# A fused attention and PReLU kernel: the order of the first loads, and which output tiles are computed in the first two stages

## The chip, the cores and the metric

The kernel runs on one core of a Trainium2 chip. The metric is the time of one execution on the device in microseconds (us), the median of several runs. TensorE is called PE, VectorE DVE, ScalarE ACT, GpSimd POOL, SyncE SP; PEld is the loading of weights into PE.

## The reference

Linear attention for 8 batches of 8 heads, 576 tokens and 64 columns a head, then a two-layer network with a learned leaky ReLU over all 4608 tokens:

```python
kv  = np.einsum('bhsd,bhse->bhde', k, v)
out = np.einsum('bhsd,bhde->bhse', q, kv)
rms = np.sqrt(np.mean(out * out, axis=-1, keepdims=True) + 1e-06)
attn = out / rms * g_norm                        # (8, 8, 576, 64)
x = attn.transpose(0, 2, 1, 3).reshape(4608, 512)
h = x @ w_in                                     # w_in (512, 2048)
g = np.maximum(h, 0.0) + alpha * np.minimum(h, 0.0)
y = g @ w_out                                    # w_out (2048, 512)
```

Everything comes and goes as float32; inside, the matmuls take 16-bit values.

## The kernel before

**Blocks and units.** The 4608 tokens are cut into nine blocks (w) of W = 512. For a block the hidden layer has NF = 16 units (g) of 128 hidden columns. A unit (`m1_group`) is four 128x512 matmuls into one PSUM bank (`m1_mm`, over the four 128-row pieces of x) and an evacuation (`m1_evac`): ACT writes relu(-h), DVE combines it with h into `gt`. The output of a block has four tiles (a) of 128 tokens; each is a chain of 16 matmuls, one for each g (`y_mm`), and `y_out` copies it out of PSUM and has SP issue two stores.

**Heads and batches.** A batch has 576 tokens, so blocks and batches don't line up: block 1 takes the last 64 tokens of batch 0 and 448 of batch 1, block 2 the last 128 of batch 1 (the "tail") and 384 of batch 2. q, k and v arrive by POOL's queue, each in two loads (`load`: the long one with five rows a partition, the short one with four), changed to 16 bits on the way. `regroup` puts heads side by side. `step_kv` makes kv for two or four pairs of heads: five matmuls of 128x128 for each pair.

**Two ways to make x.** Blocks 0 and 1 keep x with the columns on the partitions: `step_t` transposes q on PE, `step_ot` multiplies by kv, `ssq_mm` sums squares over a head by a matmul with a mask, ACT makes 1/rms by Ln and Exp, and `norm` multiplies on DVE. For batch 0, whose k, q and v come in halves of four heads, the second half goes in two column halves (`half_ot`, `half_ssq`). From block 2 on (NB_PE = 2) the tokens are on the partitions: `tile_a` multiplies, `tile_b` sums on DVE, `tile_c` has ACT and POOL make the factor `rg`, `tile_d` multiplies on DVE (`xrow`) and has SP transpose the result by DMA into `xm`. `phase_steps` hands these pieces out to the units of the block before, one tile a unit, with the lags between a, b and d in `lags`. The tail of batch 1 is made the first way (`step_tail_ot`, `step_tail_ssq`) and is written straight into `xm(2)`.

**The order.** Every engine's instructions run in the order in which the source issues them (`manual_schedule`); nothing is reordered. The start, block 0 and the second stage are written out by hand. `keep_warm(n)` issues n matmuls whose result nobody reads. `load_rest` issues the weights and batch 1. In the second stage, `ahead` multiplies block 0's output tiles `ys` while block 1's x is made: three tiles are done there, of the fourth only g 0 to 3 (`LATER = 4`); its other twelve matmuls follow in block 1's units. In the main loop a unit of block w carries four matmuls of block w-1's tiles.

**PSUM.** There are eight banks: h0, h1, h2, o0, o1, o2, s, y. A tile that takes a bank waits until the last reader of the tile before has ended.

**POOL and SP.** POOL issues all loads of q, k, v and weights in its own order, between its copies and the `rg` products; `gate` copies make it wait, at units 2 and 11 of block 1, for q's transpose and for xm(2). SP issues the stores and the transposes.

Of the kernel before, what the change touches and what calls it, by code (L numbers as in the profile page):

```python
# [9 lines left out]
FP32 = mybir.dt.float32  # L10
# [7 lines left out]
def kernel(  # L18
# [11 lines left out]
    nc = tc.nc  # L30

    B, H, S, D = q.shape
# [57 lines left out]
    def zero_rest(st):  # L90
        nc.vector.memset(st[REM:P, :, TPP, :], 0.0)
# [15 lines left out]
    def load(b, nm, h0=0, h1=H):  # L107
        load_part(b, nm, True, h0, h1)
        load_part(b, nm, False, h0, h1)

    def regroup(b, nm, h0=0, h1=H, eng=None):
        (eng or nc.vector).tensor_copy(  # L112
            out=bufs[b % NBUF][nm][:, :, h0:h1, :].rearrange("p t h d -> p h t d"),
            in_=stages[b % NBUF][nm][:, h0:h1],
        )
# [12 lines left out]
    ident = const_p.tile([P, P], FP32, name="ident")  # L128
    make_identity(nc, ident[:])
    HH = H // 2  # L130
    for h0 in (0, HH):
        for nm in "qkv":
            load(0, nm, h0, h0 + HH)

    mask32 = const_p.tile([P, P], FP32, name="mask32")
# [10 lines left out]
    nc.vector.memset(eps_t[:], 1e-6)  # L146
    ident16 = const_p.tile([P, P], FP16, name="ident16")
    nc.vector.tensor_copy(out=ident16[:], in_=ident[:])

    g2col = const_p.tile([P, 1], FP32, name="g2col")  # L150
    nc.sync.dma_start(out=g2col[0:64, :], in_=g_norm[:].unsqueeze(1))
# [35 lines left out]
    def load_rest():  # L187
        for i in range(WQ):
            load_w_in(i)
        for nm in "kvq":  # L190
            zero_rest(stages[1][nm])
        load(1, "k")
        load_w_out(0)
        load(1, "q")
        load(1, "v")
        for i in range(1, WQ):
            load_w_out(i)


# [158 lines left out]
    def step_tail_ssq(i, pool):  # L358
        ot_ps, sq = ots.pop(("tail", i))
        ssq_ps = pool[0].tile([P, JT, TAIL], FP32, name="ssq_ps", tag=pool[1])  # L360
        nc.tensor.matmul(out=ssq_ps[:], lhsT=mask16[:], rhs=sq[:], start=True, stop=True)
        rstd = attn_p.tile([P, JT, TAIL], FP32, name="rstd")
        nc.scalar.activation(
            out=rstd[:], in_=ssq_ps[:], func=AF.Ln, bias=eps_t[:], scale=inv_d,
        )
        nc.scalar.activation(out=rstd[:], in_=rstd[:], func=AF.Exp, bias=0.0, scale=-0.5)
        nc.vector.scalar_tensor_tensor(
            out=xm(NB_PE)[:, i * JT : (i + 1) * JT, 0:TAIL], in0=ot_ps[:], scalar=g2col[:],
            in1=rstd[:], op0=ALU.mult, op1=ALU.mult,
        )  # L370
# [13 lines left out]
            out=qtms[b][:], in_=bufs[b % NBUF]["q"][:].rearrange("p t h d -> p (t h d)"),  # L384
        )

    n_tile = [1]

    def next_o():
        n_tile[0] += 1  # L390
# [49 lines left out]
    def phase_steps(w):  # L440


        if w >= NW:
            return []
        todo = [(b, t) for b in range(NB_PE, min(B, w + 1)) for t in range(NT)
                if (b, t) not in done and b * S + t * P < (w + 1) * W]
        done.update(todo)
        steps = []

        kv_at = {NB_PE: 3, NB_PE + 1: 6, NB_PE + 2: 2}.get(w, 0)  # L450
        n = {NB_PE: 4, NB_PE + 1: 2}.get(w, 0)
        steps += [([], [], []) for i in range(n)]

        lags = (0, 1, 3) if w == NB_PE else (0, 1, 2)
        if w in (NB_PE + 1, NB_PE + 2):
            k = [b for b, t in todo].index(w)
            todo[k:k] = [None] * (3 if w == NB_PE + 1 else 1)
        for i in range(len(todo) + lags[2]):
            a, b, d = (
                [todo[i - k]] if 0 <= i - k < len(todo) and todo[i - k] else [] for k in lags  # L460
            )
            begin = [lambda x=x: tile_b(*x) for x in b] + [lambda x=x: tile_d(*x) for x in d]
            mid = [lambda x=x: tile_c(*x) for x in b]
# [66 lines left out]
    def spread_g():  # L530
# [7 lines left out]

    O2 = (ps_o, "o2")
    keep_warm(10)  # L540
    regroup(0, "q", 0, HH)
    nc.vector.tensor_scalar(
        out=diag[0:D], in0=ident[0:D, 0:D], scalar1=g2col[0:D], scalar2=None, op0=ALU.mult,
    )
    step_t(0, 0, H_POOL[0])
    step_t(0, 1, H_POOL[1], nc.scalar)
    regroup(0, "k", 0, HH)
    load_rest()
    keep_warm(8)
    step_kv(0, 0, 2)  # L550
    keep_warm(2)
    step_ot(0, 0)
    step_ot(0, 1)
    keep_warm(1)
    regroup(0, "q", HH, H)
    ssq_mm(0, 0)
    step_t(0, 2, H_POOL[2])
    step_t(0, 3, H_POOL[0])
    alpha_ps = ps_h.tile([P, NF], FP32, name="alpha_ps", tag="h1")
    nc.tensor.matmul(  # L560
        out=alpha_ps[:], lhsT=alpha_row[:], rhs=ident[0:NF, 0:NF], is_transpose=True,
# [4 lines left out]
    nc.vector.tensor_scalar(  # L566
        out=beta_sb[:], in0=alpha_ps[:], scalar1=-1.0, scalar2=1.0, op0=ALU.mult, op1=ALU.add,
    )
    ssq_mm(0, 1)
    regroup(0, "k", HH, H)  # L570
    spread_g()
    norm(0, 0)
    keep_warm(2)
    step_kv(0, 2, 4)
    keep_warm(2)
    load_batch(2)
    half_ot(0, (ps_s, "s"))
    norm(0, 1)
    half_ot(1, (ps_y, "y"), nc.vector)
    first = [ps_h.tile([P, W], FP32, name="h_ps", tag=f"h{g}") for g in range(3)]  # L580
    first += [ps_o.tile([P, W], FP32, name="h_ps", tag=f"o{g}") for g in range(2)]
    half_ssq(0, O2)
    for g in range(4):
        m1_mm(first[g], 0, g, (0,))
    for g in range(4):
        if g == 2:
            half_ssq(1, O2)
        m1_mm(first[g], 0, g, (1,))
    for i in range(2):
        for c in (2, 3):  # L590
            for g in range(4):
                m1_mm(first[g], 0, g, (c,), slice(i * HW, (i + 1) * HW))
                if (i, c) == (1, 3):
                    m1_evac(first[g], 0, g)
        if i == 0:
            m1_mm(first[4], 0, 4, (0, 1))
    m1_mm(first[4], 0, 4, (2, 3))
    m1_evac(first[4], 0, 4)
    others = {5: (ps_s, "s"), 6: (ps_y, "y"), 7: O2, 11: (ps_o, "o0"), 12: (ps_o, "o1"),
              13: (ps_s, "s")}  # L600
    for g in range(5, NF):
        m1_group(0, g, others.get(g))

    LATER = 4
    ys = [
        ps_h.tile([P, W], FP32, name="ya", tag="h2"),
        ps_o.tile([P, W], FP32, name="yb", tag="o0"),
# [4 lines left out]
    def ahead(g0, g1, tiles=range(TPW)):  # L614
        for g in range(g0, g1):
            for a in tiles:
                if a < TPW - 1 or g < LATER:
                    y_mm(ys[a], 0, a, g)

    S_POOL = (ps_s, "s")  # L620
    O1 = (ps_o, "o1")
    regroup(1, "k")
    ahead(0, 3)
    regroup(1, "q")
    step_t(1, 0, S_POOL)
    step_t(1, 1, O1, nc.scalar)
    step_t(1, 2, H_POOL[0])
    step_t(1, 3, H_POOL[1], nc.scalar)
    ahead(3, 4, range(2))
    step_kv(1, pool=S_POOL)  # L630
    ahead(3, 4, range(2, TPW))
    step_ot(1, 0, O1)
    step_ot(1, 1, H_POOL[0])
    step_ot(1, 2, H_POOL[1], nc.vector)
    ahead(4, 5)
    ssq_mm(1, 0, S_POOL)
    ahead(5, 7)
    ssq_mm(1, 1, S_POOL)
    norm(1, 0)
    ahead(7, 9)  # L640
    step_ot(1, 3, O1, nc.vector)
    norm(1, 1)
    ssq_mm(1, 2, S_POOL)
    ahead(9, 12)
    ssq_mm(1, 3, S_POOL)
    norm(1, 2)
    regroup(2, "q")
    transpose_q(2)
    ahead(12, 13)
    step_tail_ot(0, H_POOL[1])  # L650
    ahead(13, 15)
    norm(1, 3)
    step_tail_ssq(0, S_POOL)
    ahead(15, NF)
    for a in range(TPW - 1):
        y_out(ys[a], 0, a, nc.vector if a == 1 else None)

    LOAD_G = 6
    n_group[0] = 0
    for w in range(1, NW):
        steps = phase_steps(w + 1)
        for g in range(NF):
            if g == LOAD_G and 4 < w + 2 < B:
                load_batch(w + 2)
            a, part = divmod(g, TPW)
            parts = range(part * TPW, (part + 1) * TPW)
            if w == 1:  # L670
                a, y = TPW - 1, ys[TPW - 1]
                parts = [LATER + g] if LATER + g < NF else []
            begin, mid, end = steps.pop(0) if steps else ([], [], [])
            for f in begin:
                f()
            m1_group(w, g, [H_POOL[0], S_POOL, H_POOL[2], H_POOL[1]][g % 4] if w == 1 else None)
            for f in mid:
                f()
            if 0 in parts:
                pool, tag = ((ps_y, "y"), (ps_s, "s"))[a % 2]  # L680
                y = pool.tile([P, W], FP32, name="y_ps", tag=tag)
            for gg in parts:
                y_mm(y, w - 1, a, gg)
            if NF - 1 in parts:
                y_out(y, w - 1, a)
            for f in end:
                f()
            if (w, g) == (1, 0):
                regroup(2, "k", eng=nc.gpsimd)
            if (w, g) == (1, 2):  # L690
# [63 lines left out]
```

## Time and profile before

| | |
|---|---|
| median of 7 runs | 294.23 us (293.4 to 294.68) |
| the profiled execution | 294.13 us, its span 292.0 us |
| mean granted PE clock | 0.997 |
| busy: PE, PEld, DVE, ACT, POOL | 96%, 47%, 58%, 52%, 34% |
| w_in's first quarter issued, landed | 9.30, 16.9 us |
| first h of block 0 | 17.21 us |
| first y matmul (second stage) | 31.64 us |
| first h of block 1 | 49.10 us |
| first h of block 2 | 68.86 us |
| last of batch 2's loads landed | 53.6 us |

The span is the time from the first to the last instruction; 2.1 us lie around it. The profile gives the start of each PE instruction well, but its end is modelled and overlaps the next one; distances are best taken from start to start. A line of the timeline gives start, duration, engine, line of the source, operation, output and inputs, shape, count, and in brackets the idle time ahead of it with what ended it. The chain of waits follows the last instruction back to what released it at each step.

### The profile page before, as it was taken

What the parts mean: (1) busy time and instruction counts of PE and PEld (TensorE: products, weight loads), DVE (VectorE), ACT (ScalarE), POOL (GpSimd) and SP (SyncE); (2) the same over time, 40 slices, a digit from 0 to 9 for tenths busy, and PEclk for the clock granted to TensorE, in tenths of its full rate; (3) what the DMA queues carried; (4) which work ended last, traced back from release to release, by engine and by line L of the source; (5) the groups of instructions that cost most, each with busy time, mean ns of one, the idle gap of its engine ahead of it and who ended that gap; (6) DMA issues with size and microseconds to landing.
All of it is one profiled execution on the core that took longest, in us unless ns stands there. A gap on an engine that the chain in (4) does not pass through costs nothing.

```text
span 292.0 us, 4287 instructions
## 1 busy us (share of the span) xinstructions
PE 281.0 (96%) x1551; PEld 137.7 (47%) x1551; DVE 169.3 (58%) x261; ACT 152.8 (52%) x297; POOL 99.8 (34%) x111
## 2 busy tenths in 40 slices
PE   5999989998999999999999999999999999999994
PEld 2454444543454454455445544554445444444443
DVE  4669837787667576447744864488448644444300
ACT  1558457584656565448644754466448544444210
POOL 8923410684448128324743373324003200000000
PEclk9999999999999999999999999999999999999998
DMA  7999999999899826991699179944212311212133
GB/s 89 183 208 202 199 206 198 189 197 181 127 150 183 180 29 96 204 209 25 107 206 206 41 116 173 199 56 86 50 36 56 81 36 38 48 46 48 40 72 72
DMA packets 66228, 35.54 MB, mean 122 GB/s; under 512 B 32784, under 2 KB 61728, under 8 KB 66208
## 3 DMA queue, kind: packets, MB, share of 16 engines
q0 software_dynamic: 29664, 18.35, 45.3%
q1 hardware_dynamic: 36384, 16.80, 29.0%
q8 instruction: 12, 0.20, 0.3%
q10 hardware_dynamic: 160, 0.13, 0.2%
q14 instruction: 8, 0.07, 0.1%
HBM read 36.71 MB, written 9.44 MB: 158 GB/s over the span
## 4 chain that ended last, share of the span: by engine, by line
PE 76%; DMA 15%; POOL 4%; DVE 2%; issue 1%; ACT 1%; POOLq 0%; DVEq 0%
PE y_ps L505 38%; PE h_ps L478 33%; DMA w_in_sb<-in_moe_w_in_dram 5%; DMA vst<-in_v_dram 5%; DMA w_out_sb<-in_moe_w_out_dram 4%; PE kv_ps L245 2%; PE otm_ps L397 2%; DMA xm<-xrow 1%; DVE gt L487 1%; POOL w_in_sb L165 1%; DVE xrow L430 1%; POOL qst L97 0%; DVE ss L409 0%; POOL vst L102 0%; POOL vst L97 0%
## 5 line engine op out<-in xcount | busy, mean ns | idle before, releaser
L487 DVE SCALAR_TENSOR_TENSOR gt<-m_sb,beta_sb,h_ps 128x512 f16<-128x512 f32 x144 | 105.6, 744 | 75.1 <-ACT m_sb L485 74.5
L485 ACT ACTIVATE m_sb<-h_ps 128x512 f32<-128x512 f32 x144 | 85.4, 597 | 87.6 <-PE h_ps L478 86.4
L505 PE MATMUL y_ps<-w_out_sb,gt 128*128 128x512 f16 (+1 forms) x528 | 128.8, 373 | 0.0
L478 PE MATMUL h_ps<-xm,w_in_sb 128*128 128x512 f16 x448 | 115.0, 379 | 0.8 <-DMA xm<-xrow 0.8
L505 PEld LDWEIGHTS <-gt 128*128 128x128 f16 x592 | 57.6, 98 | 64.6 <-DMA w_out_sb<-in_moe_w_out_dram 0.2
L478 PEld LDWEIGHTS <-w_in_sb 128*128 128x128 f16 x584 | 55.8, 98 | 62.1 <-issue 2.3
L421 POOL TENSOR_TENSOR rg<-ss,g_all 128x512 f32<-128x512 f32 (+1 forms) x30 | 31.3, 1042 | 78.5 <-ACT ss L419 70.5
L478 PE MATMUL h_ps<-xt,w_in_sb 128*128 128x512 f16 (+1 forms) x136 | 30.6, 366 | 0.1
L515 ACT COPY y_sb<-y_ps 128x512 f32<-128x512 f32 (+1 forms) x32 | 18.4, 576 | 15.9 <-PE y_ps L505 15.9
L409 DVE TENSOR_REDUCE ss<-sqm_sb 128x8 f32<-128x512 f32 (+1 forms) x30 | 20.5, 683 | 10.5 <-ACT sqm_sb L403 10.5
L430 DVE TENSOR_TENSOR xrow<-otm_ps,rg 128x512 f16<-128x512 f32 (+1 forms) x30 | 20.5, 682 | 3.7 <-POOL rg L421 3.7
L403 ACT ACTIVATE sqm_sb<-otm_ps 128x512 f32<-128x512 f32 (+1 forms) x30 | 17.7, 591 | 6.3 <-PE otm_ps L397 6.3
L112 POOL COPY ksb<-kst 128x2560 f16<-128x2560 f16 x6 | 13.9, 2324 | 15.7 <-DMA kst<-in_k_dram 15.7
L112 POOL COPY qsb<-qst 128x2560 f16<-128x2560 f16 x5 | 11.6, 2316 | 10.4 <-issue 10.1
L397 PEld LDWEIGHTS <-qtm 128*128 128x128 f16 x120 | 9.1, 98 | 7.2 <-DMA qtm<-qsb 0.3
L397 PE MATMUL otm_ps<-kv_sb,qtm 128*128 128x128 f16 x120 | 11.6, 219 | 0.0
L204 PE MATMUL warm_ps<-warm,mask 128*128 128x512 f16 x25 | 8.3, 471 | 3.3 <-DVE eps_t L146 3.3
L245 PEld LDWEIGHTS <-ksb 128*128 128x128 f16 x160 | 9.4, 98 | 3.9 <-issue 0.9
L245 PE MATMUL kv_ps<-vst,ksb 128*128 128x128 f16 x160 | 10.4, 219 | 0.9 <-DMA vst<-in_v_dram 0.7
L416 ACT ACTIVATE ss<-ss,eps_t 128x8 f32<-128x8 f32 (+1 forms) x30 | 9.0, 301 | 3.2 <-DVE ss L409 2.9
L513 DVE COPY y_sb<-y_ps 128x256 f32<-128x256 f32 x1 | 0.4, 426 | 13.4 <-PE y_ps L505 13.4
L249 DVE TENSOR_TENSOR kv_sb<-kv_ps,mask 128x512 f16<-128x512 f32 (+1 forms) x9 | 5.6, 627 | 3.7 <-PE kv_ps L245 3.7
(76 smaller groups left out, 135.9 us busy)
## 6 DMA issues: line engine op xcount, KB each, us to landing
out_dram<-y_sb SPq DMA_DIRECT2D x70, 128.0 KB, 2.4
kst<-in_k_dram POOLq DMA_DIRECT2D x7, 320.0 KB, 8.5
qst<-in_q_dram POOLq DMA_DIRECT2D x7, 320.0 KB, 5.0
vst<-in_v_dram POOLq DMA_DIRECT2D x7, 320.0 KB, 10.8
w_in_sb<-in_moe_w_in_dram POOLq DMA_DIRECT2D x4, 512.0 KB, 10.2
w_out_sb<-in_moe_w_out_dram POOLq DMA_DIRECT2D x4, 512.0 KB, 15.4
kst<-in_k_dram POOLq DMA_DIRECT2D x7, 256.0 KB, 9.4
qst<-in_q_dram POOLq DMA_DIRECT2D x7, 256.0 KB, 6.4
```

The source lines that it names most:

```text
L112: (eng or nc.vector).tensor_copy(out=bufs[b % NBUF][nm][:, :, h0:h1, :].rearrange("p t h d -> p h t d"), in_=stages[b % NBUF][nm][:, h0:h1],)
L245: nc.tensor.matmul(out=kv_ps[:, j - j0, :], lhsT=ks(t), rhs=vs(t), start=(t == 0), stop=(t == NT - 1),)
L397: nc.tensor.matmul(out=ot_ps[:, 2 * j : 2 * j + 2, :], lhsT=qtms[b][:, t * NPAIR + j, :], rhs=kvs[b, j], start=True, stop=True,)
L403: nc.scalar.activation(out=sq[0:n], in_=ot_ps[0:n], func=AF.Square)
L409: nc.vector.tensor_reduce(out=ss[0:n], in_=sq[0:n], op=ALU.add, axis=mybir.AxisListType.X,)
L421: nc.gpsimd.tensor_tensor(out=rg[0:n], in0=ss[0:n].unsqueeze(2).to_broadcast([n, H, D]), in1=g_all[0:n].unsqueeze(1).to_broadcast([n, H, D ...
L430: nc.vector.tensor_mul(out=x[0:n], in0=ot_ps[0:n], in1=rg[0:n])
L478: nc.tensor.matmul(out=h_ps[:, cols], lhsT=w_in_blk(c, g), rhs=xt_of(w, c)[:, cols], start=(c == 0), stop=(c == NC - 1 and cols.stop == W),)
L485: nc.scalar.activation(out=m_sb[:], in_=h_ps[:], func=AF.Relu, scale=-1.0)
L487: nc.vector.scalar_tensor_tensor(out=gt[:], in0=m_sb[:], scalar=beta_sb[:, g : g + 1], in1=h_ps[:], op0=ALU.mult, op1=ALU.add,)
L505: nc.tensor.matmul(out=y[:], lhsT=gts[w, g][:, a * P : (a + 1) * P], rhs=w_out_blk(g)[:, cols], start=(g == 0), stop=(g == NF - 1),)
L515: nc.scalar.copy(out=y_sb[:, cols], in_=y[:])
```

## The change

- q of batch 0 is loaded whole and ahead of k and v, which still come in halves. All four pairs of q are transposed at the start, the second and the fourth evacuated by ACT. alpha and g are prepared ahead of kv.
- The rows of the second stage buffers that no load writes are zeroed by DVE at the start rather than inside `load_rest`.
- `load_rest` loads two quarters of w_out ahead of batch 1, and then k, q, v. Before, one quarter stood between k and q.
- 19 warm-up matmuls instead of 25. The order of the pieces of batch 0 shifts: kv of the second half comes ahead of the first norm, the second column half is squared on ACT and not on DVE, and units 4 and 5 of block 0 begin early.
- In the second stage all four tiles of block 0 are finished. Block 1 no longer carries a remainder of block 0; from its unit 2 on it carries one matmul a unit of its own first tile, 14 in all. Block 2 carries the other 50 of block 1, spread evenly.
- In block 1 the three tiles of batch 2 stand two units apart, with lags (0, 1, 4) for (0, 1, 3). The tail moves from the second stage into block 1, after units 9, 11 and 13, its last product in a function of its own (`tail_norm`). POOL's regroup of q of batch 3 and its second gate move one unit later.

The diff, cut to its core:

```diff
+    load(0, "q")
     for h0 in (0, HH):
-        for nm in "qkv":
+        for nm in "kv":
             load(0, nm, h0, h0 + HH)
...
+    for nm in "qkv":
+        zero_rest(stages[1][nm])
...
     def load_rest():
         for i in range(WQ):
             load_w_in(i)
-        for nm in "kvq":
-            zero_rest(stages[1][nm])
-        load(1, "k")
         load_w_out(0)
-        load(1, "q")
-        load(1, "v")
-        for i in range(1, WQ):
+        load_w_out(1)
+        for nm in "kqv":
+            load(1, nm)
+        for i in range(2, WQ):
             load_w_out(i)
...
-        lags = (0, 1, 3) if w == NB_PE else (0, 1, 2)
+        lags = (0, 1, 4) if w == NB_PE else (0, 1, 2)
+        if w == NB_PE:
+            todo = [x for t in todo for x in (t, None)][:-1]
...
+    regroup(0, "q", 0, HH)
+    regroup(0, "q", HH, H)
     step_t(0, 0, H_POOL[0])
     step_t(0, 1, H_POOL[1], nc.scalar)
     regroup(0, "k", 0, HH)
-    load_rest()
-    keep_warm(8)
-    step_kv(0, 0, 2)
-    keep_warm(2)
-    step_ot(0, 0)
-    step_ot(0, 1)
-    keep_warm(1)
-    regroup(0, "q", HH, H)
-    ssq_mm(0, 0)
     step_t(0, 2, H_POOL[2])
-    step_t(0, 3, H_POOL[0])
+    step_t(0, 3, (ps_o, "o0"), nc.scalar)
...
-    ssq_mm(0, 1)
+    spread_g()
+    load_rest()
+    keep_warm(2)
+    step_kv(0, 0, 2)
+    keep_warm(2)
+    step_ot(0, 0)
+    step_ot(0, 1)
     regroup(0, "k", HH, H)
-    spread_g()
+    keep_warm(2)
+    ssq_mm(0, 0)
+    ssq_mm(0, 1, H_POOL[2])
+    step_kv(0, 2, 4)
     norm(0, 0)
-    keep_warm(2)
-    step_kv(0, 2, 4)
-    keep_warm(2)
+    keep_warm(3)
     load_batch(2)
     half_ot(0, (ps_s, "s"))
     norm(0, 1)
-    half_ot(1, (ps_y, "y"), nc.vector)
+    half_ot(1, (ps_y, "y"))
...
     regroup(1, "q")
+    ahead(3, 6)
     step_t(1, 0, S_POOL)
...
+    ahead(6, 7)
     step_kv(1, pool=S_POOL)
+    ahead(7, 8)
     step_ot(1, 0, H_POOL[0])
     step_ot(1, 1, O1)
     step_ot(1, 2, H_POOL[1], nc.vector)
...
+    ahead(11, QW)
+    ahead(QW, NF, (0,))
     ssq_mm(1, 3, S_POOL)
     norm(1, 2)
     regroup(2, "q")
     transpose_q(2)
+    y_out(ys[0], 0, 0)
+    ahead(QW, NF, (1,))
     norm(1, 3)
+    ahead(QW, NF, (2,))
+    y_out(ys[1], 0, 1, nc.vector)
+    y_out(ys[2], 0, 2)
+    ahead(QW, NF, (3,))
+    y_out(ys[3], 0, 3)
...
+    AHEAD = NF - 2
...
             if w == 1:
-                a, y = TPW - 1, ys[TPW - 1]
-                parts = [LATER + g] if LATER + g < NF else []
+                parts = [(0, g - NF + AHEAD)] if g >= NF - AHEAD else []
+            else:
+                n0 = AHEAD if w == 2 else 0
+                n1, d = TPW * NF - n0, 2 * (w == 2)
+                cut = lambda i: max(0, (n1 + d) * i // NF - d)
+                parts = [divmod(n0 + i, NF) for i in range(cut(g), cut(g + 1))]
...
+            if (w, g) == (1, 9):
+                step_tail_ot(0, next_o())
+            if (w, g) == (1, 11):
+                step_tail_ssq(0, next_o())
+            if (w, g) == (1, 13):
+                tail_norm(0)
...
-            if (w, g) == (1, 8):
+            if (w, g) == (1, 9):
                 regroup(3, "q", eng=nc.gpsimd)
-            if (w, g) == (1, 11):
+            if (w, g) == (1, 12):
                 nc.gpsimd.tensor_copy(out=gate[:], in_=xm(2)[0:1, 0, W - 1 : W])
                 load(3, "v")
```

More of the change, by code (lines that the diff above doesn't have):

```diff
@@ L366, in step_tail_ssq, with tail_norm @@
         nc.scalar.activation(out=rstd[:], in_=rstd[:], func=AF.Exp, bias=0.0, scale=-0.5)
+        ots["tail", i] = (ot_ps, rstd)
+    def tail_norm(i):
+        ot_ps, rstd = ots.pop(("tail", i))
         nc.vector.scalar_tensor_tensor(
@@ L385, in transpose_q @@
         )
-    n_tile = [1]
+    n_tile = [2]
     def next_o():
@@ L540 @@
     keep_warm(10)
-    regroup(0, "q", 0, HH)
     nc.vector.tensor_scalar(
@@ L578 @@
     norm(0, 1)
-    half_ot(1, (ps_y, "y"), nc.vector)
+    half_ot(1, (ps_y, "y"))
     first = [ps_h.tile([P, W], FP32, name="h_ps", tag=f"h{g}") for g in range(3)]
     first += [ps_o.tile([P, W], FP32, name="h_ps", tag=f"o{g}") for g in range(2)]
+    m1_mm(first[0], 0, 0, (0,))
+    m1_mm(first[1], 0, 1, (0,))
     half_ssq(0, O2)
+    m1_mm(first[2], 0, 2, (0,))
+    m1_mm(first[3], 0, 3, (0,))
     for g in range(4):
[L584 to L587, printed above, removed]
         m1_mm(first[g], 0, g, (1,))
+    half_ssq(1, O2)
+    m1_mm(first[4], 0, 4, (0, 1))
     for i in range(2):
@@ L595 @@
         if i == 0:
[L596 to L599, printed above, removed]
+            first.append(ps_s.tile([P, W], FP32, name="h_ps", tag="s"))
+            m1_mm(first[5], 0, 5, (0, 1))
+    for g in (4, 5):
+        m1_mm(first[g], 0, g, (2, 3))
+        m1_evac(first[g], 0, g)
+    others = {6: (ps_y, "y"), 7: O2, 11: (ps_o, "o0"), 12: (ps_o, "o1"),
               13: (ps_s, "s")}
-    for g in range(5, NF):
+    for g in range(6, NF):
         m1_group(0, g, others.get(g))
-    LATER = 4
     ys = [
@@ L616, in ahead @@
             for a in tiles:
-                if a < TPW - 1 or g < LATER:
-                    y_mm(ys[a], 0, a, g)
+                y_mm(ys[a], 0, a, g)
     S_POOL = (ps_s, "s")
     O1 = (ps_o, "o1")
+    QW = NF - GW
     regroup(1, "k")
@@ L628 @@
     step_t(1, 3, H_POOL[1], nc.scalar)
-    ahead(3, 4, range(2))
+    ahead(6, 7)
     step_kv(1, pool=S_POOL)
-    ahead(3, 4, range(2, TPW))
-    step_ot(1, 0, O1)
-    step_ot(1, 1, H_POOL[0])
+    ahead(7, 8)
+    step_ot(1, 0, H_POOL[0])
+    step_ot(1, 1, O1)
     step_ot(1, 2, H_POOL[1], nc.vector)
-    ahead(4, 5)
+    ahead(8, 9, range(2))
     ssq_mm(1, 0, S_POOL)
-    ahead(5, 7)
+    ahead(8, 9, range(2, TPW))
+    ahead(9, 10)
     ssq_mm(1, 1, S_POOL)
     norm(1, 0)
-    ahead(7, 9)
-    step_ot(1, 3, O1, nc.vector)
+    ahead(10, 11)
+    step_ot(1, 3, H_POOL[0])
     norm(1, 1)
     ssq_mm(1, 2, S_POOL)
-    ahead(9, 12)
+    ahead(11, QW)
+    ahead(QW, NF, (0,))
     ssq_mm(1, 3, S_POOL)
@@ L648 @@
     transpose_q(2)
-    ahead(12, 13)
-    step_tail_ot(0, H_POOL[1])
-    ahead(13, 15)
+    y_out(ys[0], 0, 0)
+    ahead(QW, NF, (1,))
     norm(1, 3)
[L653 to L656, printed above, removed]
+    ahead(QW, NF, (2,))
[3 more added lines that the diff above has]
+    y_out(ys[3], 0, 3)
     LOAD_G = 6
-    n_group[0] = 0
+    n_group[0] = 1
+    AHEAD = NF - 2
     for w in range(1, NW):
@@ L667 @@
                 load_batch(w + 2)
-            a, part = divmod(g, TPW)
-            parts = range(part * TPW, (part + 1) * TPW)
             if w == 1:
-                a, y = TPW - 1, ys[TPW - 1]
-                parts = [LATER + g] if LATER + g < NF else []
+                parts = [(0, g - NF + AHEAD)] if g >= NF - AHEAD else []
[4 more added lines that the diff above has]
+                parts = [divmod(n0 + i, NF) for i in range(cut(g), cut(g + 1))]
             begin, mid, end = steps.pop(0) if steps else ([], [], [])
@@ L675 @@
                 f()
-            m1_group(w, g, [H_POOL[0], S_POOL, H_POOL[2], H_POOL[1]][g % 4] if w == 1 else None)
+            m1_group(w, g, [H_POOL[1], S_POOL, H_POOL[2], H_POOL[0]][g % 4] if w == 1 else None)
             for f in mid:
                 f()
[L679 to L685, printed above, removed]
+            for a, gg in parts:
+                if gg == 0:
+                    pool, tag = ((ps_y, "y"), (ps_s, "s"))[a % 2]
+                    y = pool.tile([P, W], FP32, name="y_ps", tag=tag)
+                wy = w if w == 1 else w - 1
+                y_mm(y, wy, a, gg)
+                if gg == NF - 1:
+                    y_out(y, wy, a)
             for f in end:
                 f()
+            if (w, g) == (1, 9):
[4 more added lines that the diff above has]
+                tail_norm(0)
             if (w, g) == (1, 0):
```

## The prediction

> **What bounds the kernel now.** I read the page's busy shares, then PE's timeline up to 70 us, then its waits, then the chain of waits. The share (PE 96%) is too coarse: matmul records overlap, so I count from start to start. A warm 128x512 matmul takes 0.216 us (ya 31.64, yb 31.86, yc 32.07), a 128x128 one 0.056 us (20 of L245 take 1.11 us from first start to next start).
>
> After 69.7 us the waits view of PE and of PEld lists nothing: from there the end is a count of matmuls. Everything open lies earlier. PE's timeline, with bracketed idle time and its releaser (the lines where a stage begins or PE waits):
>
> ```profile
> 17.21 1.46 PE L478 MATMUL h_ps<-xt,w_in_sb 128*128 128x512 f16 x6
> ...
> 31.64 0.38 PE L505 MATMUL ya<-w_out_sb,gt 128*128 128x512 f16 x1
> ...
> 34.90 1.29 PE L221 MATMUL qt_ps<-ident,qsb 128*128 128x128 f16 x20 [0.51 <-DVE qsb L112]
> ...
> 37.11 1.28 PE L245 MATMUL kv_ps<-vst,ksb 128*128 128x128 f16 x20 [0.48 <-DMA vst<-in_v_dram]
> ...
> 39.17 0.80 PE L278 MATMUL ot_ps<-qt_sb,kv_sb 128*128 128x448 f16 x5 [0.33 <-DVE kv_sb L249]
> ...
> 53.77 1.28 PE L245 MATMUL kv_ps<-vst,ksb 128*128 128x128 f16 x20 [0.19 <-DMA vst<-in_v_dram]
> ...
> 68.86 1.02 PE L478 MATMUL h_ps<-xm,w_in_sb 128*128 128x512 f16 x4 [0.81 <-DMA xm<-xrow]
> ```
>
> A record ends about 0.16 us after the next could start, so a stall is the bracket plus 0.16: 0.67, 0.65, 0.5, 0.35 and (two full unit steps after 66.79 give 67.66) 1.2 us, 3.4 us in all. All five wait, directly or through a copy, for data. The chain shows why, from the first weight to v of batch 2:
>
> ```profile
> 11.63 14.34 DMA w_in_sb<-in_moe_w_in_dram
> 25.97 0.28 issue
> 26.25 12.97 DMA w_out_sb<-in_moe_w_out_dram
> 39.22 0.28 issue
> 39.50 14.13 DMA vst<-in_v_dram
> 53.64 0.14 issue
> 53.77 1.28 PE kv_ps L245 x20
> ```
>
> The loads stand in one line and each goes at some 205 GB/s; POOL issues a load when the eighth before it has landed. Until 53.6 us the order of loads decides what PE can do.
>
> **What the Trainium skill says.** "TensorE: Matmul & The Clock Gate", Part 1: 426.7 ns from start to start cold, 215.7 ns warm, warm after about 3.4 us of work, cold again after an idle window of that length. The trace agrees with both figures: ten warm-ups take 4.22 us from 3.26, eight take 1.89 us from 7.88. "DMA: Bandwidth & Descriptors", Anatomy of one DMA: about 2.0 us fixed plus bytes / 436e3; the first 160 KB would be an estimated 2.4 us, and measured 3.4 from issue, so I use landings from the trace. "Trainium Kernel Development and Optimization", Key Constraints: DMAs of all queues share the same 16 engines. The three transposes into xm fit that: under loads and behind one another they took 5.6 to 3.4 us, later single ones 2.4.
>
> **The change part by part.**
>
> *Start.* q whole ahead of k and v changes the order of 1.77 MB, not the amount: 10 issues instead of 12, about 1.2 us of POOL saved, but DMA already moves 150 to 200 GB/s, so at most a few tenths. Landings by bytes ahead (at 9.73 us, 0.88 MB had landed): q whole 7.9 us, k's first half 9.7, v's 11.3 (was 9.7), v's second 14.4 (was 14.5). So q's transposes start 1.2 us later and kv of the first half 1.6 us later. From there: kv 0.56, kv_sb 0.42 with 0.2 us of hand-over, ot 0.2 and square 0.55, then ACT in a row, 2 x (Ln 0.69 + Exp 0.63) from 14.1, squares to 17.8, Ln and Exp of the halves: the second half of xt at 21.4 instead of 21.2. PE is not held up by that, since it now has blocks of g 4 and 5 ahead of the halves. What holds PE are w_in's first quarters, 16.9 and 19.5 us before; their bytes ahead are the same. From the second quarter there are 56.5 matmuls left, 12.2 us: y begins at about 31.5 (31.64). I take -0.1, bounds -0.4 and +0.4. The memsets of the second stage buffers (3 x 0.27 us of DVE) fall in DVE's idle time before q. Six warm-up matmuls fewer cost nothing in PE time, which waits there anyway; whether the clock survives it is a rival below.
>
> *Second stage.* w_out's second quarter goes ahead of batch 1 (0.52 MB, 2.6 us): w_out 28.6 and 31.2, k 33.8, q 36.4, v 39.2, then w_out 41.8 and 45 as before. In exchange PE has 24 y matmuls (5.2 us, up to 36.7) ahead of q's transposes, not 12. q is regrouped (0.81) by 37.3: stall 0.6. Transposes 1.1, one g 0.86: 39.3, v is there. kv 1.1, one g 0.86, kv_sb ready 0.95 after kv: stall 0.1. The third w_out is wanted at 42.1, the fourth at 46.4: both landed. The chain ssq, Ln, Exp, norm (about 2.4 us) is covered by 11 matmuls (2.4). Before: 17.46 us for 52 y, 40 small, 10 full ones (15.6), stalls 1.9. After: 64 y 13.8, 40 small 2.2, 4 ot and 4 ssq 1.7, sum 17.7, stalls 0.7: block 1 begins at 31.5 + 18.4 = 49.9 (49.10). Four y_out instead of three lie on ACT and DVE and on SP's queue (8 issues of about 0.6 us, behind q's transpose of 4.84); the first consumer of that queue after them comes 5 us later.
>
> *Block 1.* Its 64 h matmuls 13.8, 14 y of its own first tile 3.0 (12 of the old fourth tile before), kv 1.1, three tiles 0.65, tail 0.43 moved in: 19.0. v of batch 2 (53.6) is wanted at 53.8, so its 0.35 stall goes. What is late next is the last transposed tile. Its multiply (xrow) moves from unit 9 to unit 12, so it has four units behind it, 4.3 us of PE, instead of seven. Before, POOL gave rg only at 59.16 to 63.18 because four DMA issues stood ahead, and the three transposes queued up:
>
> ```profile
> 62.11 4.41 SPq L435 DMA_TRANSPOSE xm<-xrow  x3
> ...
> 65.30 3.42 DMA xm<-xrow
> 68.72 0.14 issue
> 68.86 1.02 PE h_ps L478 x4
> ```
>
> Two units apart and with lag 4, rg is ready and each transpose runs alone. Unit 12 begins at 64.6; the evacuation of unit 11 (ACT 0.6, DVE 0.75 and hand-over) goes first, xrow 65.7 to 66.4. For the landing I take 3.0 (2.4 alone, 3.4 before; 5.6 is the upper bound): 69.4. PE is done at 68.9, stall 0.5. tail_norm, now behind unit 13 (0.75 us of DVE), ends about 68.8. So block 2 begins at 69.4, not 68.86. On POOL, q of batch 3 is regrouped a unit later, behind the third rg; its transpose on SP still follows xm's, as before (67.89, landed 7.9 us later), and its first reader comes at about 81. POOL's gate for v of batch 3 waits for the same tile, and kv(3) is 10 us later: covered. The banks change hands (o2, o0, o1 in turn, h from four), each evacuated a unit or more before its next writer.
>
> *From there.* 14 y matmuls are done ahead: 14 x 0.216 = 3.0 us less. Block 2's units hold 3.25 y instead of 4 (1.56 us). DVE needs 2.1 us in the two or three units with a reduce and an xrow: less than 1 us behind, three banks of h cover it. xm of block 3 landed 3.1 us ahead of need; 1.3 remains.
>
> Sum against the profiled execution (294.13 us, span 292.0): 69.4 - 68.86 - 3.0 = -2.5. For hand-overs of a tenth that no row shows I give back 0.3: -2.2, span 289.8, time 291.9; the median of the runs is 0.1 above that execution, so **292.0**. Another way round: stalls 3.4 become 1.2.
>
> **The rivals.** A measurement tells about 0.2% (0.6 us) from no change.
> 1. Forecast, 0.68: 292.0, from 291.0 (no stall at block 2, start -0.4) to 293.2 (start +0.4, q later by 0.5, landing 3.4).
> 2. The clock, 0.10: between 7.5 and 17 us PE is only about half busy with six warm-ups fewer and a gap of 1.1 us ahead of q. For it: the trace was warm only after 7 us. Against: no gap of 3.4 us. Price: one cold window at the start of h, 3.4 us at half speed, 1.7 us lost, of which the wait for q gives 0.6 back, and up to 0.9 us for a slower start chain: 293.1 to 294.0.
> 3. The loads move the stall, 0.08: batch 1 lands 1.3 us later than reckoned, because it now competes with more w_out in flight: PE waits at the transposes, 293.3.
> 4. Slower, 0.14: the last transposed tile. At its upper bound, 0.7 us of DVE backlog at unit 12 and 5.6 us to landing, xm is there at 72.7, PE waits 3.8 us, and 72.8 - 68.86 - 3.0 = +0.9: 295.2. It decides from a landing at 71.9 on (5.5 us after xrow instead of 3.0). For it: the first of the three took 5.6. Against: that was under the loads of batch 3, which (1.2 MB from about 57) are through by 64.
>
> **How the numbers follow.** Faster: nearly all of 1, half of 2, three quarters of 3: 0.77. Same: 0.08. Slower: case 4 and a sliver of 2: 0.15. The range reaches from the good end of 1 to most of case 4, 291.0 to 294.9.
>
> **What would show it.** PE's timeline after: first h near 17.0, y near 31.5, transposes of q near 37.3 with about half a us of idle, no wait at kv of batch 2, block 2 near 69.4, then no idle. Wrong if warm-ups or h after 8 us stand 0.43 apart, if block 2 begins after 71.9, or if PE waits again after it, at xm of block 3 above all.

## The result and the profile after

The changed kernel takes 291.66 us (median of 12 runs, 291.3 to 292.5) against 294.15 us for the kernel before (31 runs): a ratio of 0.9913, 95% interval 0.9899 to 0.9927, or 2.5 us less. The profiled execution took 291.55 us, its span is 289.4 us.

PE's timeline after, at the same places (start, duration, engine, line, operation, count, and in brackets the idle time ahead with its releaser):

```profile
16.23 0.61 PE L485 MATMUL h_ps<-xt,w_in_sb 128*128 128x512 f16 x2 [0.53 <-DMA w_in_sb<-in_moe_w_in_dram]
...
30.89 0.38 PE L512 MATMUL ya<-w_out_sb,gt 128*128 128x512 f16 x1
...
36.67 1.29 PE L222 MATMUL qt_ps<-ident,qsb 128*128 128x128 f16 x20 [0.43 <-DVE qsb L112]
...
38.84 1.28 PE L246 MATMUL kv_ps<-vst,ksb 128*128 128x128 f16 x20
...
49.55 2.75 PE L485 MATMUL h_ps<-xt,w_in_sb 128*128 128x512 f16 x12
...
53.44 1.28 PE L246 MATMUL kv_ps<-vst,ksb 128*128 128x128 f16 x20
...
69.37 1.02 PE L485 MATMUL h_ps<-xm,w_in_sb 128*128 128x512 f16 x4 [0.60 <-DMA xm<-xrow]
```

kv of batch 1, the first ot after it and kv of batch 2 have lost their brackets. Two waits of note are left after y begins: 0.6 us for q of batch 1 (0.43 and the 0.16 by which a record overlaps the next) and 0.75 us for the last transpose into xm; with 0.2 us ahead of kv of batch 1 they are 1.5 us. After block 2's first h the waits view of PE lists nothing. v of batch 2 has gone from the chain of waits; the longest load in it is now the one that ends with q of batch 1:

```profile
19.00 16.70 DMA qst<-in_q_dram
35.78 0.84 DVE qsb L112
36.67 1.29 PE qt_ps L222 x20
...
66.15 3.08 DMA xm<-xrow
69.24 0.14 issue
69.37 1.02 PE h_ps L485 x4
```

The steps of the prediction beside what came of them (us from the start of the span):

| | before | predicted | after |
|---|---|---|---|
| first y matmul | 31.64 | 31.5 | 30.89 |
| q's transposes, batch 1 | 34.90 | 37.3 | 36.67 |
| kv of batch 1 | 37.11 | 39.3 | 38.84 |
| block 1 | 49.10 | 49.9 | 49.55 |
| block 2 | 68.86 | 69.4 | 69.37 |
| y matmuls of block 1 left at block 2 | 64 | 50 | 50 |
| waits of PE from the first y to block 2 | 3.4 | 1.2 | 1.5 |
| span | 292.0 | 289.8 | 289.4 |

### The profile page after: what moved, and what is told of

It is laid out like the page before. It is cut to its first block, busy times and chain, and to the rows that moved or that the text cites. A ratio compares the mean times of both kernels' runs of the same rounds, so it can differ in the third digit from the quotient of the medians.

```text
span 289.4 us, 4268 instructions
## 1 busy us (share of the span) xinstructions
PE 279.4 (97%) x1545; PEld 137.0 (47%) x1545; DVE 166.1 (57%) x256; ACT 154.4 (53%) x300; POOL 99.4 (34%) x109
## 4 chain that ended last, share of the span: by engine, by line
PE 81%; DMA 12%; DVE 2%; ACT 2%; POOL 1%; issue 1%; POOLq 0%; DVEq 0%; ACTq 0%
PE y_ps L512 37%; PE h_ps L485 35%; DMA qst<-in_q_dram 8%; DMA w_in_sb<-in_moe_w_in_dram 3%; PE kv_ps L246 3%; PE otm_ps L402 2%; DMA xm<-xrow 1%; DVE gt L494 1%; ACT m_sb L492 1%; PE yd L512 1%; PE yc L512 1%; PE ya L512 1%; PE yb L512 1%; DVE ss L414 1%; PE qt_ps L222 0%
## 5 line engine op out<-in xcount | busy, mean ns | idle before, releaser
L512 PE MATMUL y_ps<-w_out_sb,gt 128*128 128x512 f16 (+1 forms) x528 | 131.1, 373 | 0.0
L112 POOL COPY ksb<-kst 128x2560 f16<-128x2560 f16 x6 | 13.9, 2324 | 16.2 <-DMA kst<-in_k_dram 16.2
L205 PE MATMUL warm_ps<-warm,mask 128*128 128x512 f16 x19 | 7.0, 510 | 3.3 <-DVE eps_t L147 3.3
L232 ACT COPY qt_sb<-qt_ps 128x576 f16<-128x576 f16 x4 | 2.4, 639 | 12.7 <-PE qt_ps L222 12.7
```

Source lines behind the costliest of these rows:

```text
L112: (eng or nc.vector).tensor_copy(out=bufs[b % NBUF][nm][:, :, h0:h1, :].rearrange("p t h d -> p h t d"), in_=stages[b % NBUF][nm][:, h0:h1],)
L512: nc.tensor.matmul(out=y[:], lhsT=gts[w, g][:, a * P : (a + 1) * P], rhs=w_out_blk(g)[:, cols], start=(g == 0), stop=(g == NF - 1),)
```

## The experiments

Each ratio is to the kernel before on the same chip in the same session. With 291.66 us, 0.9913 is the number to set beside.

| run | us, median | ratio, 95% interval |
|---|---|---|
| start_alone | 294.14 | 0.9994 (0.9984 to 1.0003) |
| start_undone | 292.51 | 0.9942 (0.9927 to 0.9958) |
| q_halves_first | 292.11 | 0.9932 (0.9915 to 0.9948) |
| load_order_alone | 295.73 | 1.0042 (1.0029 to 1.0056) |
| w_out_late | 296.24 | 1.0063 (1.0047 to 1.0079) |
| dense_tiles | 291.95 | 0.9910 (0.9878 to 0.9941) |
| k3_late | 295.21 | 1.0023 (1.0006 to 1.0040) |
| k3_short_late | 292.65 | 0.9950 (0.9933 to 0.9967) |
| fill_three | 291.30 | 0.9905 (0.9886 to 0.9925) |
| fill_six | 292.14 | 0.9923 (0.9902 to 0.9944) |
| k3_short_fill | 295.22 | 1.0031 (1.0014 to 1.0048) |
| no_fillers | 291.99 | 0.9909 (0.9875 to 0.9943) |

### Why everything at the start came 0.7 us early

**q_halves_first.** The one edit:

```diff
-    load(0, "q")
+    for h0 in (0, HH):
+        load(0, "q", h0, h0 + HH)
```

> The changed kernel, q of batch 0 still ahead of k and v but in its two halves of heads (12 loads ahead of w_in, not 10). Theory A (the rate rises because the first loads are fewer and larger): bytes moved by 13 us fall back by some 0.12 MB, w_in's first quarter lands near 16.9 and the time goes up by 0.5 to 0.7, to 292.3. Theory B (it is the order, q's transposes out of the way, not the rate): 291.7.

Measured: 292.11 us, 0.45 above the change; theory A had 0.5 to 0.7, theory B nothing. The two intervals overlap, so the traces have to decide. The windows view (length, busy time of each engine, PE clock, DMA share, GB/s in the last column), first before, then after, then with q in halves:

```profile
5.00:10.00 5.00, 4.95 (x29) 2.28 (x28) 2.68 (x7) 0.64 (x1) 4.67 (x8) 1.00 1.24 160
10.00:13.00 3.00, 2.66 (x27) 1.43 (x24) 1.16 (x3) 1.52 (x3) 2.85 (x5) 1.00 1.37 188
```

```profile
5.00:10.00 5.00, 4.25 (x29) 2.06 (x28) 2.16 (x5) 0.99 (x2) 4.41 (x7) 1.00 1.40 194
10.00:13.00 3.00, 2.90 (x20) 1.38 (x21) 1.45 (x5) 0.83 (x3) 2.98 (x5) 1.00 1.40 197
```

```profile
5.00:10.00 5.00, 3.41 (x29) 1.92 (x27) 1.44 (x3) 0.72 (x2) 4.39 (x8) 1.00 1.26 164
10.00:13.00 3.00, 2.20 (x18) 1.17 (x18) 1.59 (x5) 0.56 (x1) 2.99 (x5) 1.00 1.39 195
```

From 5 to 10 us the loads move 194 GB/s with q whole and 160 to 164 with q in halves, whatever stands first. All ten profiles with q whole show 194 to 196 in this window, the four with q in halves 153 to 166. From 0 to 5 us q whole is behind (45 GB/s against 59 and 58). Over the first 15 us it has moved 0.14 MB more than before and 0.10 MB more than with q in halves, which at 205 GB/s is 0.7 and 0.5 us. w_in's first quarter landed at 16.2 us with q whole, at 16.9 before and at 17.1 with q in halves; y begins at 30.89, 31.64 and 31.77.

So it is not the order of the loads but q's loads being larger and fewer. The two are not told apart: with q in halves POOL has two more issues ahead of w_in, and w_in's first quarter goes out at 9.61 us, not at 8.72. Why the rate is higher, with pieces of the same length, the runs don't tell.

**start_alone** is the kernel before with the new start only: q whole and first, the change's sequence of steps up to block 0, and `load_rest` called where the change calls it, with its loads in the old order.

```diff
-    for h0 in (0, HH):
-        for nm in "qkv":
+    load(0, "q")
+    for h0 in (0, HH):
+        for nm in "kv":
             load(0, nm, h0, h0 + HH)
...
-    regroup(0, "q", 0, HH)
...
+    regroup(0, "q", 0, HH)
+    regroup(0, "q", HH, H)
...
-    load_rest()
...
+    spread_g()
+    load_rest()
...
```

> The kernel before with the new start only (q whole and first, all four q transposes early, the new order of batch 0's pieces); load order after w_in, second stage and block 1 as before. Theory (in the changed kernel the loads run at some 195 GB/s from 5 us on instead of some 165, so every later landing is 0.7 us earlier): all waits down to v of batch 2 move by 0.7 us, y begins at 30.9, block 2 at 68.2; 293.4 to 293.6. Rival (the gain is the reordered second stage, and the start only lets PE wait longer for loads that land as before): y begins earlier but batch 1's q and v land as before; 294.0 to 294.3.

Measured 294.14 us, no difference that can be told: the theory's number was wrong. The rival's number came, but not for the rival's reason, since batch 1 did land earlier (q's transposes at 34.28, kv at 36.46). The stages came 0.5 to 0.65 us early (y at 31.12, block 1 at 48.45, kv of batch 2 at 53.28), but not block 2:

```profile
68.82 1.02 PE L479 MATMUL h_ps<-xm,w_in_sb 128*128 128x512 f16 x4 [1.25 <-DMA xm<-xrow]
```

It begins at 68.82 against 68.86, and the idle time there has grown from 0.81 to 1.25 us. The early start went into the wait for xm. **start_undone** is the other half, the changed kernel with the old start (the same hunks turned round):

```diff
-    load(0, "q")
     for h0 in (0, HH):
-        for nm in "kv":
+        for nm in "qkv":
             load(0, nm, h0, h0 + HH)
...
```

> The changed kernel with the old start (q, k, v in halves of heads, 25 warm-ups), everything after it as changed. Theory: y begins at 31.6, q of batch 1 lands 0.7 us later, block 2 begins at 70.0; 292.3 to 292.5. Rival (start worth nothing): 291.7.

Measured 292.51 us, the time that the theory gave (its y begins at 31.95, block 2 at 69.70, where it had 31.6 and 70.0). By the medians the start is worth 0.1 us by itself and some 0.8 us on top of the rest; the profiled executions show only 0.3 us of the 0.8 (block 2 at 69.70 against 69.37). The parts don't add: in all four kernels block 2 begins when xm is there, and not when PE is.

### The order of the loads and the four whole tiles

**load_order_alone** puts only the new order of `load_rest` into the kernel before:

```diff
-        load(1, "k")
         load_w_out(0)
-        load(1, "q")
-        load(1, "v")
-        for i in range(1, WQ):
+        load_w_out(1)
+        for nm in "kqv":
+            load(1, nm)
+        for i in range(2, WQ):
             load_w_out(i)
```

**w_out_late** takes only the second quarter of w_out back behind batch 1 in the changed kernel:

```diff
         load_w_out(0)
-        load_w_out(1)
         for nm in "kqv":
             load(1, nm)
-        for i in range(2, WQ):
+        for i in range(1, WQ):
             load_w_out(i)
```

> The kernel before with the new order in load_rest only (two quarters of w_out, then k, q, v of batch 1). Theory (the early w_out is worth something only with the y matmuls that eat it, since batch 1 lands 2.5 us later): PE stands some 3 us at q's transposes instead of 0.67, kv of batch 1 starts at 39.3 instead of 37.1, part of it comes back at kv of batch 2 and at xm; 295.4 to 296.2. Rival (order of the loads counts for nothing): 294.2.

> The changed kernel with the second quarter of w_out loaded behind batch 1's v instead of ahead of batch 1's k; the second stage still asks for it at its g 4 and 5. Theory (the early quarter is what feeds PE while batch 1 arrives): w_out's second quarter lands near 38.5 instead of 29.7, PE stands still from about 34.4 to 38.7, and of this some 2.6 us come back because q and v are there by then; 292.5 to 293.5. Rival (only the number of bytes counts): 291.7.

Each is slower than before, by 1.3 and 2.0 us. load_order_alone came out as expected: 295.73 us, 2.87 us idle at q's transposes (37.77), block 2 at 70.42. w_out_late was slower than expected by some 3 us, and PE's timeline shows the reason:

```profile
38.67 0.38 PE L511 MATMUL ya<-w_out_sb,gt 128*128 128x512 f16 x1 [4.09 <-DMA w_out_sb<-in_moe_w_out_dram]
...
39.55 0.63 PE L511 MATMUL ya<-w_out_sb,gt 128*128 128x512 f16 x1
39.97 0.63 PE L511 MATMUL yb<-w_out_sb,gt 128*128 128x512 f16 x1
40.40 0.63 PE L511 MATMUL yc<-w_out_sb,gt 128*128 128x512 f16 x1
40.83 0.63 PE L511 MATMUL yd<-w_out_sb,gt 128*128 128x512 f16 x1
41.25 2.08 PE L221 MATMUL qt_ps<-ident,qsb 128*128 128x128 f16 x20
```

PE stood still for 4.3 us, worked for 0.9, and then the matmuls stand 0.43 apart, not 0.216, nearly up to 43.2 us: the clock fell to half (the granted clock is 0.50 from 39.5 to 41.2 us). The 24 matmuls of that stretch, 2.0 us at full speed, took 3.6. One of the 21 executions has a mean granted clock of 1.0 and took 294.43 us; the others have 0.985 to 0.994 and took 295.6 to 297.3. The expectation had the gap and not the clock, and it had "some 2.6 us come back", while only the two waits for q and v (0.8 us) were there to give back. Loads and tiles are one edit: the tiles are the work that the early weights feed, and either without the other costs time.

### What block 2 waits for

**dense_tiles** sets the three tiles of batch 2 one unit apart again, lags (0, 1, 3):

```diff
-        lags = (0, 1, 4) if w == NB_PE else (0, 1, 2)
-        if w == NB_PE:
-            todo = [x for t in todo for x in (t, None)][:-1]
+        lags = (0, 1, 3) if w == NB_PE else (0, 1, 2)
```

> The changed kernel with the three tiles of batch 2 one unit apart and lags (0, 1, 3) as before the change; the tail, the loads and the gates as changed. Theory (the loads of batch 3 hold the transposes back until about 66, whenever they are issued): three issues between 60 and 64, landing near 68.5, 291.4 to 291.7, so the spacing brought nothing by itself. Rival (the spacing is what keeps rg, xrow and the transposes from queuing): landing later than 69.2, 292 and more.

**k3_late** moves a load:

```diff
                 load(3, "q")
-                load(3, "k")
...
                 nc.gpsimd.tensor_copy(out=gate[:], in_=xm(2)[0:1, 0, W - 1 : W])
+                load(3, "k")
                 load(3, "v")
```

> The changed kernel, k of batch 3 loaded behind POOL's second gate (with v) and no longer behind the first (with q). Theory (the transposes into xm make no headway while batch 3's loads run, so block 2's begin hangs on the end of those loads): the loads beside the transposes are halved and through near 61, each transpose lands some 2.5 us after its issue, the third near 68.7; PE waits 0.1 to 0.3 us, 291.1 to 291.2. Rival (a transpose takes 3 us by itself or waits for its issue): third still at 69.2, 291.7; slower if k of batch 3 is now late for its kv.

Measured: 291.95 us for dense_tiles, not to be told from the change by its interval, and between its two forecasts; 295.21 us for k3_late. The view of xm from 58 to 70 us gives the issues of the three transposes (duration of the issue in ns, first and last start) and their times to landing, first after, then dense_tiles, then k3_late:

```profile
L440 SPq DMA_TRANSPOSE xm<-xrow x3: 1189/1190/1203, 61.3 to 66.2; - x3
...
DMA to landing us min/median/max: 3.1/4.9/6.9
```

```profile
L440 SPq DMA_TRANSPOSE xm<-xrow x3: 1200/1216/1227, 61.9 to 64.5; - x3
...
DMA to landing us min/median/max: 5.2/6.0/6.9
```

```profile
L440 SPq DMA_TRANSPOSE xm<-xrow x3: 1190/1190/1204, 61.3 to 66.2; - x3
...
DMA to landing us min/median/max: 2.4/2.4/4.4
```

In dense_tiles the last transpose was issued 1.7 us earlier and landed no earlier (64.5 + 5.2 = 69.7, against 66.15 + 3.1). In k3_late, issued at the same times as in the change, but with half of the loads beside them, the second and third took 2.4 us, and block 2 began without a wait at 68.72. What DMA moved from 63 to 66 us, with POOL's loads as q0 and SP's queue as q1 (packets, MB, share of the 16 engines), first after, then k3_late, where q0 has nothing:

```profile
q0 software_dynamic: 921, 0.52, 121.4%
q1 hardware_dynamic: 201, 0.08, 18.0%
```

```profile
q1 hardware_dynamic: 807, 0.19, 97.0%
```

So the transposes make hardly any headway while batch 3's loads run, which ends at about 66 us (the rate falls from 202 GB/s to 58 there). Then they land one behind the other, half a microsecond apart: at 68.2, 68.7 and 69.2 in the change. The third was issued when the loads were all but through and still took 3.08 us, not 2.4. That is what absorbed the early start in start_alone too: there the last one was issued 1.06 us earlier than before and took 4.45 us instead of 3.42. Why it gained nothing at all there, with the loads themselves some 0.6 us earlier, is not settled.

k3_late lost more elsewhere: k and v of batch 3 now came too late for their kv.

```profile
81.05 1.62 PE L246 MATMUL kv_ps<-vst,ksb 128*128 128x128 f16 x20 [2.01 <-DMA vst<-in_v_dram]
```

k, the other operand, landed at 77.46 and was regrouped on POOL until 79.8; the two waits overlap. PE stood still for 2.2 us, and 0.9 us after it went on its clock fell to half, until 85.3 us:

```profile
82.46 1.49 PE L512 MATMUL y_ps<-w_out_sb,gt 128*128 128x512 f16 x3
83.74 1.76 PE L485 MATMUL h_ps<-xm,w_in_sb 128*128 128x512 f16 x4
```

Three y matmuls take 1.28 us from start to start here, 0.65 at full speed. The slow stretch costs 1.7 us and the gap 2.2, while 0.75 us were saved at block 2: 3.1 of the 3.4 us between the two profiled executions. The clock did not fall every time. Of the 22 executions 12 have a mean granted clock of 0.993 or 0.994, with a median of 295.5 us; the other 10 have 0.997 to 1.0, with a median of 294.3. Without the clock k3_late would still lose. It was the clause after the semicolon in the expectation that came true. dense_tiles has no wait at xm left, but because block 1 itself is longer: DVE falls behind in three tiles in a row, a y matmul that asks for the unit two back waits 0.82 us for its gt at 62.55, and tail_norm starts at 68.94 instead of 67.74. PE comes to block 2 at 69.8 with nothing gained. The spacing keeps DVE even; it is not what brings xm earlier.

**k3_short_late** puts only k's short load behind the second gate:

```diff
                 load(3, "q")
-                load(3, "k")
+                load_part(3, "k", True)
...
+                load_part(3, "k", False)
                 load(3, "v")
```

> The changed kernel; of k of batch 3 only the short load (256 KB of the 1.15 MB) goes behind POOL's second gate. Theory (the transposes are held back by the loads beside them, to the end of those): the loads are through 1.3 us earlier, near 64.6, the third transpose takes 2.4 to 2.6 us from its issue at 66.1 and lands near 68.7, PE waits about 0.1 us, and k of batch 3 is regrouped before 76, in time for its kv at 79; 291.0 to 291.2. Rival (what remained is the duration of the transpose, not the loads): 291.7.

Measured 292.65 us, slower than the change. The first half of the theory came true (third transpose 2.4 us, block 2 at 68.86). kv of batch 3 then waited (0.95 us for v, at 80.13), since k was regrouped at 75.44 as expected but v had moved back with it; and xm of block 3 was late by 0.63 us.

### Filling the wait

**fill_three** and **fill_six** (`FILL` 3 and 6) put y matmuls that are due anyway ahead of block 2's first h, and take them out of the units where they stood; **k3_short_fill** is k3_short_late and fill_three together:

```diff
...
+            if (w, g) == (2, 0):
+                y1 = ps_s.tile([P, W], FP32, name="y_ps", tag="s")
+                for gg in range(FILL):
+                    y_mm(y1, 1, 1, gg)
             m1_group(w, g, ...)
...
```

> The changed kernel, three y matmuls of block 1's second tile (g 0 to 2) moved ahead of block 2's first h, where PE waits for the last transpose into xm. Theory (the wait of 0.76 us at block 2 is a pure idle of PE and all after it is a count of matmuls): three times 0.216 fill it, 291.0 to 291.1, with 0.1 us left of the wait. Rival (a later wait takes its place, at xm of block 3 or for PSUM): 291.6.

> As fill_three, with six y matmuls of block 1's second tile ahead of block 2's first h. With three, 0.68 us of the wait were left, since the last transpose landed no earlier and PE had come to it earlier. Theory (a pure idle of PE): three more fill 0.65 us, 290.7 to 290.9. Rival (the landing moves on with PE, or something later waits): 291.3.

> k3_short_late and fill_three together. Theory: the wait at block 2 is gone already with three matmuls, 290.9 to 291.0, as far as fill_six gets; nothing is added up beyond that, because PE then has no idle left after kv of batch 1. Rival (two separate waits): 290.5.

fill_three: 291.30 us, 0.36 below the change, less than expected and within the intervals of both; xm landed at 69.44 and left 0.52 us of idle time. fill_six: 292.14 us. Block 2 begins at 70.14, straight behind seven y matmuls in a row (from 68.62), without a wait, which was the aim. But:

```profile
97.30 1.04 PE L485 MATMUL h_ps<-xm,w_in_sb 128*128 128x512 f16 x4 [1.46 <-DMA xm<-xrow]
```

Block 3 now waits for its own xm: its last two transposes took 5.5 and 4.4 us instead of 3.3 and 2.4. Two stores of a tile now stand between the transposes in SP's order (at 90.5 us, behind them in the change), but they do so in fill_three too (at 90.2), without a wait. What differs is the loads of batch 4 beside the transposes: from 91 to 94 us they move 0.10 MB in the change, 0.13 in fill_three and 0.28 in fill_six; in k3_short_late, which has the stores behind and yet waits, they move 0.43 MB. It fits what was seen at block 2, but no run varies this alone.

k3_short_fill, 295.22 us, shows the same wait at 2.11 us, with 0.42 MB of loads from 91 to 94 us; neither of its forecasts had that. Its executions fall into two groups of 11: mean granted clock 0.999 or 1.0 and 293.2 to 295.1 us (the profiled one is of these), or 0.993 to 0.994 and 295.3 to 296.8 us. Its median lies between them. In fill_six the rival "something later waits" was right. No variant that ran is clearly faster than the change.

### The clock

**no_fillers** leaves out the nine `keep_warm` matmuls after the first ten:

```diff
-    keep_warm(2)
     step_kv(0, 0, 2)
-    keep_warm(2)
     step_ot(0, 0)
...
-    keep_warm(2)
     ssq_mm(0, 0)
...
-    keep_warm(3)
     load_batch(2)
```

> The changed kernel with only the first ten warm-up matmuls; the nine between the pieces of batch 0 are left out. Theory (the clock stays up[...], and PE waits there anyway): 291.7, h from its start 0.216 apart. Rival (the fillers hold the clock): h starts 0.43 apart[...], 292.5 to 293.4.

Measured 291.99 us (291.4 to 292.4), not to be told from the change. In the profiled execution, though, the clock was down:

```profile
8.42 2.31 PE L222 MATMUL qt_ps<-ident,qsb 128*128 128x128 f16 x20 [0.74 <-DVE qsb L112]
...
11.88 1.23 PE L246 MATMUL kv_ps<-vst,ksb 128*128 128x128 f16 x10 [0.32 <-DVE g_all L543]
...
33.29 0.38 PE L512 MATMUL ya<-w_out_sb,gt 128*128 128x512 f16 x1
```

Twenty transposes take 2.31 us (1.29 at full speed), and the clock comes up only at about 19 us; y begins 2.4 us later. PE then met no wait at all down to the end: the three waits of the change took up 1.5 us of it, and block 2 began at 70.30, 0.9 us later. (The view's granted clock reads 1.00 over this stretch, as it does over the slow first warm-ups; it is read from the distances of the matmuls.)

That the missing fillers began this is not shown. The clock was still down at 8.42, ahead of the first filler. In the other profiles with this start it was up before these transposes or came up during them (1.29 to 1.71 us for the twenty), also ahead of the first filler. So the ten warm-ups alone don't always do, and one profile can't tell whether fillers would have ended the slow stretch sooner. For the fillers speaks that four of the six executions have a mean granted clock of 0.987 to 0.994, and all twelve of the change 0.997 or more; in the times it does not show.

## Why the prediction was right, and where its terms were off

- **The whole.** 292.0 us was forecast, 291.66 came. The sum that was worked out, 2.5 us, is what was measured; the 0.3 us given back "for hand-overs of a tenth that no row shows" stood for nothing. That the sum fits so well is in part luck, as the next points say. (The 67.66 in the prediction is one unit of four h after 66.79, not two; the 1.2 us that follow from it are right.)
- **The start was mis-sized.** "So at most a few tenths", -0.1 with bounds of 0.4, was -0.75. The step that failed is "changes the order of 1.77 MB, not the amount": the rate changed, from 160 to 194 GB/s between 5 and 10 us, and q_halves_first ties it to q's loads being larger and fewer. The windows of before held the hint: 160 GB/s in that stretch and 205 later. At block 2 hardly any of it shows (69.37 against 69.4 forecast), because block 2 waits for its transposes and not for PE.
- **Second stage.** The exchange went as worked out, about 0.6 us earlier throughout: q regrouped at 36.6 (37.3), wait 0.6 (0.6), kv at 38.84 (39.3). The wait ahead of the first ot did go. load_order_alone and w_out_late show that neither side of the exchange stands alone. The moved tail and the 14 early y matmuls were not run by themselves.
- **v of batch 2** was covered, as said.
- **The last transpose.** Landed at 69.24, forecast 69.4, so the stage's end was right. The reason was half wrong: "the loads of batch 3 ... are through by 64" should read 66, and "each transpose runs alone" failed: the first took 6.9 us and the second 4.9. The landing hangs on the end of the loads and, as far as the spacing of the three landings shows, on the two transposes then still ahead, not on when rg is ready. The 3.0 us taken between two other figures met the 3.08 measured by luck. PE was there at 68.6, not 68.9, so the wait was 0.75, not 0.5.
- **From there.** No wait after block 2, 14 matmuls fewer, 3.0 us: right. The margin "1.3 remains" at xm of block 3 was the next weak point: fill_six, k3_short_late and k3_short_fill ran into it.
- **The rivals.** The clock held in the changed kernel's profile. The profile of no_fillers shows what a slow start costs: about as reckoned at y (2.4 against 1.7 plus up to 0.9), but more of it is swallowed (1.5, not 0.6). "Against: no gap of 3.4 us" was no safeguard: in k3_late the clock fell after 2.2 us of idle time. Batch 1 came earlier, not later. The slower case needed a landing after 71.9; it was 69.2, and 69.7 in dense_tiles.

Measured, the 2.6 us between the two spans are 0.75 from the earlier y and 1.9 from waits (3.4 to 1.5). That is where the time shows, not what each edit is worth: start_alone and start_undone give 0.1 and, by the medians, 0.8 us for the same edit.

## What to carry to other kernels

Where loads stand in one line and PE is nearly full, an edit's worth is decided at the next place where PE waits for something that the edit doesn't move: list those places in order and carry the shift through each. Move loads and the work that eats them together, and look at what the moved load pushes back: each of the three attempts to free block 2's transposes made a kv or the next block's transposes late. Where the rate in an early window lies below the later one, look at the size and number of the loads, and not only at their order. Reckon a wait of two microseconds or more on PE at more than its length, since the clock may fall behind it; and where the times of a kernel fall into two groups, look at the granted clock of each execution.

## What the runs showed of the hardware that was not expected

- A DMA transpose of 128 x 512 elements took 2.4 us with little beside it and up to 7.6 us beside loads on POOL's queue (fill_three). Three issued 1.2 to 2.5 us apart all landed within about 1 us of one another, half a microsecond apart, once the loads had ended.
- The same bytes in the same pieces: 194 to 196 GB/s with q in loads of 320 and 256 KB, 153 to 166 GB/s with q in loads of 160 and 128 KB, in the same five microseconds.
- After 4.3 us of idle time (w_out_late) and after 2.2 us (k3_late) PE ran 0.9 us at full speed before the clock fell, and then some 3.5 us at or near half. After 3.0 us (load_order_alone) and 2.3 us (k3_short_fill) it stayed up in the profiled executions; but 7 of 18 and 11 of 22 executions of these two have a mean granted clock of 0.993 or 0.994, and the medians of these lie 0.9 and 1.9 us above those of the rest.
